# Keys of the last sixteen chunks transposed in blocks by VectorE, another form of the activation, and input buffers of its own for the fourth chunk

## The chip, the cores and the metric

One core of one Trainium2 chip runs the kernel. The metric is the device time of an execution in microseconds: the median of three runs of the kernel before is 521.48 us (521.38 to 521.93). Engines are named as in the profile: PE is TensorE (matmul; PEld is its weight load), DVE is VectorE, ACT is ScalarE, POOL is GpSimd, SP is SyncE, which issues all DMAs here. L452 is line 452 of the kernel.

## The reference

Two stages. For each of 4 batches and 8 heads a recurrence runs over 768 steps with a state of 48x48; its outputs, 3072 tokens of 384 values, go through two matrices of 384x2048 and 2048x384 with the activation h * tanh(softplus(h)) between them.

```python
f = 1.0 / (1.0 + np.exp(-f_logit))
for t in range(S):
    state = f[:, :, t, :, None] * state + np.einsum('bhd,bhe->bhde', k[:, :, t], v[:, :, t])
    y[:, :, t] = np.einsum('bhd,bhde->bhe', q[:, :, t], state)
...
h = x @ w_in
sp = np.where(h > 20.0, h, np.log1p(np.exp(np.minimum(h, 20.0))))
g = h * np.tanh(sp)
return (g @ w_out).astype(np.float32)
```

## The kernel before, in words

**Attention.** The recurrence is done in 24 chunks of 128 steps; chunk n is of batch n % 4. Heads are padded to 64 and lie in four pairs (`NP`), so keys, queries and decays of a chunk are each a tile of 128 partitions (two heads) by 4 x 128. A chunk goes through four steps. `load` and `prep` (L363 to L408) fetch decays, keys, queries and values by four DMAs of 256 KB, turn the decay logits into cumulative sums (by matmuls with a triangle, L391, for chunks 0 to 3, by a scan on VectorE, L396, for the others) and scale keys and queries. `attn0` makes the scores inside half chunks (L427). `attn1` (L446) transposes the scaled keys, four 128x128 transposes on TensorE into a bank of PSUM (L452) and a copy by ScalarE into `kt` (L455). `attn2` (L457) multiplies the transposed keys by the values (L470), keys as the weights, 32 matmuls of 64x64 in four tiles of the array (16 in the last four chunks), and adds that to the state; from chunk 4 on the scores follow in the same step of TensorE. `attn3` (L490) makes the outputs (L505, L517) and splits them into a high part and a low part in `xt`. For chunks 0 to 3 the low part is made by subtracting the high part in PSUM with a matmul (L546) and copying the rest by ScalarE (L548); for the others by a VectorE subtraction (L550). Some rows of `xt` are then moved to other partitions by DMA (L556).

Input buffers come in rings of three (`NR`), chunk n uses number n % 3. So the loads of chunk 3 wait until chunk 0 has been through.

**The two matrices.** Four chunks make a group of 512 tokens. A unit is one group and one of 16 slices of 128 hidden values: 96 units. A unit has 9 matmuls of 512 columns for h (L247, weights and x each as high and low part), the activation, and two units later 9 matmuls (L270) into three accumulators `o`. The first two groups are done in half turns of 8 slices each (`TURNS`), with their sums kept in DRAM between; the weights arrive as 64-bit numbers, are put together by integer operations and split into two parts in `split_w` (L342 to L360), 8 slices before unit 8, the other 8 from unit 16 on.

**The activation** (`mish`, L253) works on 128x512 values. With u = exp(h), taken as exp(10 - relu(10 - h)), it forms n = u(u + 2) and h * n / (n + 2), the division as exp(-ln(n + 2)): relu, exp, ln, exp and a copy for the high part on ScalarE, three operations on VectorE (L259, L260, L263), the low part on GpSimd (L265).

**Order.** Nothing is issued in program order. `Plan` collects all steps with an engine, an estimated cost, what they read and write, and for DMAs a size. `order` packs them by these estimates, with ranks from a backward pass, and applies a fixed list of random nudges to the ranks (`SEEDS`); then each engine gets its instructions in the order of the planned starts, SP's DMAs too. An engine takes its queue strictly in that order. `attend_goal` (with `LEAD`) says which attention steps are put in beside which unit: chunks 4 to 7 beside units -4 to 4, chunks 8 to 11 beside units 24 to 32, and from there four chunks beside each 16 units. Until the first output step TensorE gets fill matmuls (L339) where the plan has it idle. At the end a check (L593) counts decays that are too small; if there are any, a slow version runs behind it, which is not executed with these inputs.

Of the kernel before, what the change touches and what calls it, by code (L numbers as in the profile page):

```python
# [35 lines left out]
H_CAP = 10.0  # L36
# [11 lines left out]
]  # L48
NR = 3
LAG = 2  # L50


class Plan:
# [12 lines left out]
    def add(self, engine, cost, issue, reads=(), writes=(), size=0, port=False):  # L66
# [11 lines left out]
        self.steps.append((engine, cost, issue, before, size, port or engine == "pool"))  # L78

    def pack(self, rank, ahead, haste, back=False):  # L80
# [19 lines left out]
        for _ in range(count):  # L100
# [21 lines left out]
            for a in after[i]:  # L122
                f = a if back else i
                if engine[i] == engine[a] == "pe":
                    lag = 0.0
                else:
                    lag = self.LATENCY[engine[f]]
                    if back and engine[f] == "sp":
                        lag += steps[f][4] / 0.32
# [73 lines left out]
def recurrence_moe_kernel(  # L203
# [29 lines left out]
    two = ctile([P, 1], F32, "two")  # L233
    hcap = ctile([P, 1], F32, "hcap")
# [40 lines left out]
    with tc.tile_pool(name="work", bufs=1) as pool, tc.tile_pool(  # L275
# [17 lines left out]
        at_, h_, o_ = (ring(nm, n, [P, GT], F32, psum) for nm, n in (("at", 3), ("h", 2), ("o", NK)))  # L293
        halves = [dram.tile([DM, GT], F32, tag=f"half{g}", name=f"half{g}") for g in range(2)]
# [14 lines left out]
        def consts():  # L309
# [6 lines left out]
            nc.gpsimd.memset(two, 2.0)  # L316
            nc.gpsimd.memset(hcap, H_CAP)
            nc.gpsimd.memset(ones, 1.0)

# [42 lines left out]

        def load(n, parts):  # L363
            i = n % NR
            st = NP // parts
            for s in range(0, NP, st):
                for nm, dst, src in (("l", l_, ft if n < NS else fl), ("k", k_, kk), ("q", q_, qq)):
                    add("sp", 500, lambda dst=dst, src=src, s=s: nc.sync.dma_start(  # L368
                        dst[i][:, s : s + st], src[n][:, s : s + st]),
                        (), pairs((nm, i), range(s, s + st)), 65.5 * st)  # L370
            add("sp", 500, lambda: nc.sync.dma_start(v_[i], vn[n]), (), [("v", i)], 262)

        def prep(n, parts):
            i = n % NR

            taken[n] = b, keys = banks()
            f, k, q, end = l_[i], k_[i], q_[i], ends[:, n]
            st = NP // parts
            for s0 in range(0, NP, st):
# [3 lines left out]
                kf, kk_, kq = (pairs((x, i), ps) for x in "lkq")  # L383
# [21 lines left out]
                times(0 < n < 2 * GC, w, k[:, s], k[:, s], inv, ki, kk_, port=n < 2 * GC)  # L405
# [410 lines left out]
```

## Time and profile before

| | |
|---|---|
| median of 3 runs | 521.48 us (521.38 to 521.93) |
| span of the profiled execution, from first to last instruction | 519.1 us |
| outside the span, against the median | 2.4 us |
| mean granted clock of TensorE | 0.992 |
| busy: TensorE, VectorE, ScalarE, GpSimd | 505.9, 366.7, 416.4, 156.1 us |
| DMA | 48.86 MB, 94 GB/s |

The profiled execution's own time is its span and what lies before the first and behind the last instruction; the runs that were timed lie within 0.55 us of each other. Matmuls are pipelined, and their ends in the profile are modelled, so the steps between starts, as the chain of waits has them, say more than a matmul's own duration: a matmul of 512 columns is shown with some 400 ns, but nine of them follow each other in 2.10 us.

### The profile page before, as it was taken

Reading aid. Unit: us, or ns where it says so; the run is one execution under the profiler, and the core shown is the slowest. Engines: PE = TensorE matmul, PEld = TensorE weight load, DVE = VectorE, ACT = ScalarE, POOL = GpSimd, SP = SyncE. Lnnn points to the kernel's source line nnn. Section 1 sums busy time; section 2 is a strip of 40 time slices with the busy share of each in tenths; the row PEclk is TensorE's granted clock in tenths of the full one; section 3 lists DMA queues with packets and bytes.
Section 4 is the critical chain, followed back from the end, with each engine's and each line's share of the span. In section 5 each row is a group of like instructions: output and inputs, shape, how many; then the busy total and the mean of one; then the engine's idle time right before and its main releaser. Section 6 shows DMA issues by size and latency. Waiting matters only on the chain.

```text
span 519.1 us, 12812 instructions
## 1 busy us (share of the span) xinstructions
PE 505.9 (97%) x5250; PEld 399.9 (77%) x5250; DVE 366.7 (71%) x592; ACT 416.4 (80%) x731; POOL 156.1 (30%) x134
## 2 busy tenths in 40 slices
PE   8799999999999999999999999999999999999995
PEld 6677777777787778778778778778787787878884
DVE  3679999999997876856767667665668564545451
ACT  6698988988999888888778788877778786777771
POOL 1142443333332223232233232323232221232322
PEclk9799999999999999999999999999999999999999
DMA  8977634524601533320213321130210000010001
GB/s 257 346 227 265 218 125 152 158 87 142 221 25 38 189 102 111 124 59 27 82 40 92 104 82 43 45 101 10 74 49 1 4 2 32 2 60 0 1 1 66
DMA packets 22625, 48.86 MB, mean 94 GB/s; under 512 B 2656, under 2 KB 3808, under 8 KB 22560
## 3 DMA queue, kind: packets, MB, share of 16 engines
q1 hardware_dynamic: 22560, 47.98, 28.2%
q8 instruction: 42, 0.69, 0.5%
q14 instruction: 23, 0.19, 0.1%
HBM read 39.32 MB, written 6.29 MB: 88 GB/s over the span
## 4 chain that ended last, share of the span: by engine, by line
PE 85%; DVE 5%; ACT 3%; DMA 2%; issue 2%; SPq 1%; POOL 0%; DVEq 0%; ACTq 0%
PE h L247 37%; PE o L270 36%; PE at L517 2%; PE at L505 2%; PE at L470 2%; PE at L427 2%; PE at L452 2%; DMA raw<-ww 1%; DMA l<-fl 1%; DVE wt L356 1%; SPq L368 1%; PE o L339 1%; DVE n L259 1%; DVE wt L354 1%; DVE g L263 1%
## 5 line engine op out<-in xcount | busy, mean ns | idle before, releaser
L265 POOL TENSOR_TENSOR gl<-g,gh 128x512 fp32r<-128x512 f32 x96 | 128.9, 1344 | 292.9 <-ACT gh L264 257.0
L247 PE MATMUL h<-xt,wh 128*128 128x512 f32 x576 | 185.0, 402 | 1.2 <-DVE g L263 1.2
L247 PEld LDWEIGHTS h<-xt,wh 128*128 128x128 f32 x576 | 105.2, 188 | 27.7 <-DVE g L263 2.9
L270 PE MATMUL o<-gh,wh 128*128 128x512 f32 x288 | 116.0, 403 | 0.0
L247 PE MATMUL h<-xt,wl 128*128 128x512 f32 x288 | 113.7, 395 | 0.0
L270 PE MATMUL o<-gh,wl 128*128 128x512 f32 x288 | 113.7, 395 | 0.0
L270 PE MATMUL o<-gl,wh 128*128 128x512 f32 x288 | 113.7, 395 | 0.0
L259 DVE SCALAR_TENSOR_TENSOR n<-n 128x512 f32<-128x512 f32 x96 | 67.9, 707 | 54.6 <-ACT n L258 54.2
L257 ACT ACTIVATE n<-h,hcap 128x512 f32<-128x512 f32 x96 | 65.7, 685 | 32.6 <-PE h L247 31.9
L263 DVE TENSOR_TENSOR g<-g,h 128x512 f32<-128x512 f32 x96 | 65.4, 682 | 36.8 <-ACT h L262 36.2
L261 ACT ACTIVATE h<-n,two 128x512 f32<-128x512 f32 x96 | 65.9, 686 | 18.6 <-DVE g L260 17.5
L264 ACT ACTIVATE gh<-g 128x512 fp32r<-128x512 f32 x96 | 60.1, 627 | 19.3 <-DVE g L263 14.1
L260 DVE TENSOR_TENSOR g<-h,n 128x512 f32<-128x512 f32 x96 | 66.2, 690 | 9.3 <-POOL gl L265 1.3
L258 ACT ACTIVATE n<-n,hcap 128x512 f32<-128x512 f32 x96 | 69.2, 721 | 2.3
L270 PEld LDWEIGHTS o<-gh,wh 128*128 128x128 f32 x288 | 54.0, 187 | 13.7 <-issue 0.3
L270 PEld LDWEIGHTS o<-gl,wh 128*128 128x128 f32 x288 | 54.0, 187 | 13.2
L247 PEld LDWEIGHTS h<-xt,wl 128*128 128x128 f32 x288 | 54.0, 187 | 13.2
L270 PEld LDWEIGHTS o<-gh,wl 128*128 128x128 f32 x288 | 54.1, 188 | 12.0
L262 ACT ACTIVATE h<-h 128x512 f32<-128x512 f32 x96 | 55.8, 582 | 1.7
L396 DVE TENSOR_TENSOR_SCAN cum<-go,l 128x512 f32<-128x512 f32 x20 | 26.9, 1343 | 0.9 <-ACT l L388 0.8
L433 DVE TENSOR_TENSOR a<-at,causal 128x256 f32<-128x256 f32 x44 | 17.6, 418 | 10.5 <-PE at L427 10.5
L533 POOL TENSOR_TENSOR state<-tmp,ends 128x256 f32<-128x256 f32 x20 | 16.0, 802 | 24.8 <-PE at L505 16.9
(103 smaller groups left out, 500.6 us busy)
## 6 DMA issues: line engine op xcount, KB each, us to landing
raw<-ww SPq DMA_DIRECT2D x16, 768.0 KB, 4.9
v<-vn SPq DMA_DIRECT2D x24, 256.0 KB, 3.7
k<-kk SPq DMA_DIRECT2D x23, 256.0 KB, 3.0
q<-qq SPq DMA_DIRECT2D x23, 256.0 KB, 3.7
l<-fl SPq DMA_DIRECT2D x20, 256.0 KB, 2.7
out<-ob SPq DMA_DIRECT2D x18, 256.0 KB, 2.9
xt<-xt SPq DMA_DIRECT2D x15, 128.0 KB, 2.1
half<-ob SPq DMA_DIRECT2D x6, 256.0 KB, 2.2
```

The source lines that it names most:

```text
L247: nc.tensor.matmul(h, w[:, j, a * P : (a + 1) * P], xt[:, x, a, :], start=(n == 0), stop=(n == 3 * NK - 1))
L257: ("act", T_ACT(GT, True, 1), 0, lambda: nc.scalar.activation(u, h, AF.Relu, bias=hcap, scale=-1.0)),
L258: ("act", T_ACT(GT, False, 1), 0, lambda: nc.scalar.activation(u, u, AF.Exp, bias=hcap, scale=-1.0)),
L259: ("dve", T_DVE(GT), 1, lambda: nc.vector.scalar_tensor_tensor(n, u, 2.0, u, ALU.add, ALU.mult)),
L260: ("dve", T_DVE(GT), 0, lambda: nc.vector.tensor_tensor(g, h, n, ALU.mult)),
L261: ("act", T_ACT(GT, False, 1), 0, lambda: nc.scalar.activation(h, n, AF.Ln, bias=two)),
L262: ("act", T_ACT(GT, True), 0, lambda: nc.scalar.activation(h, h, AF.Exp, scale=-1.0)),
L263: ("dve", T_DVE(GT), 0, lambda: nc.vector.tensor_tensor(g, g, h, ALU.mult)),
L264: ("act", T_ACT(GT), 0, lambda: nc.scalar.activation(gh, g, AF.Copy)),
L265: ("pool", T_POOL(GT), 1, lambda: nc.gpsimd.tensor_tensor(gl, g, gh.bitcast(F32), ALU.subtract)),
L270: nc.tensor.matmul(o, w[:, j, m * P : (m + 1) * P], x, start=(first and i == 0), stop=(last and i == 2))
L396: add("dve", 2 * T_DVE(w) - 70, lambda s=s, cum=cum: nc.vector.tensor_tensor_scan(cum.rearrange("p a c -> p (a c)"), go[:, s].rearrange("p ...
```

## The change

- From chunk 8 on (`TD`), `attn1` has VectorE transpose the keys in blocks of 32x32 into the tile `inv` (free by then), stores that to DRAM (`kd`) and loads it back into `kt` by four DMAs, one for every 32 steps, each of 128 runs of 512 bytes. In `kt` the channels of a pair now lie four values (16 bytes) apart, and the update reads them so (`mixed`). The four transposes on TensorE and the ScalarE copy go for these chunks.
- The activation is h * (1 - 2r) with r = 1 / ((1 + u)^2 + 1): exp, clamp and add 1, square, ln, exp, one product. The product made is h * (r - 0.5), and the factor -2 is applied where the accumulators `o` are copied or added. The square is done by ScalarE for units 0 to 29 and by VectorE from unit 30 on (`SQ_DVE`).
- Chunk 3 is loaded into `ob` (output buffers) and one of the `g` tiles, and from chunk 4 on the ring starts anew with buffer 0 (`slot`, `place`).
- The low parts of chunks 0 to 3 are made by VectorE as those of the others (`LO_PE` is empty).
- The steps are packed anew, with a list of 24 nudges in place of 48. A step can have a lag of its own; none has one.

The core of the diff:

```diff
-H_CAP = 10.0
+U_CAP = 22026.46484375
...
 SEEDS = [
...
 NR = 3
+LO_PE = ()
+K_POOL = (1, 2, 3, 4, 5, 6, 7)
 LAG = 2
+TD = 8
+SQ_DVE = range(30, 96)
...
-    def add(self, engine, cost, issue, reads=(), writes=(), size=0, port=False):
+    def add(self, engine, cost, issue, reads=(), writes=(), size=0, port=False, lag=None):
...
-    def mish(h, n, g, gh, gl):
-
-        u = n
+    def mish(h, n, g, gh, gl, on_dve=False):
+
+
+        square = (
+            ("dve", T_DVE(GT), 1, lambda: nc.vector.tensor_tensor(n, n, n, ALU.mult)) if on_dve else
+            ("act", T_ACT(GT), 0, lambda: nc.scalar.activation(n, n, AF.Square))
+        )
         return (
-            ("act", T_ACT(GT, True, 1), 0, lambda: nc.scalar.activation(u, h, AF.Relu, bias=hcap, scale=-1.0)),
-            ("act", T_ACT(GT, False, 1), 0, lambda: nc.scalar.activation(u, u, AF.Exp, bias=hcap, scale=-1.0)),
-            ("dve", T_DVE(GT), 1, lambda: nc.vector.scalar_tensor_tensor(n, u, 2.0, u, ALU.add, ALU.mult)),
-            ("dve", T_DVE(GT), 0, lambda: nc.vector.tensor_tensor(g, h, n, ALU.mult)),
-            ("act", T_ACT(GT, False, 1), 0, lambda: nc.scalar.activation(h, n, AF.Ln, bias=two)),
-            ("act", T_ACT(GT, True), 0, lambda: nc.scalar.activation(h, h, AF.Exp, scale=-1.0)),
-            ("dve", T_DVE(GT), 0, lambda: nc.vector.tensor_tensor(g, g, h, ALU.mult)),
+            ("act", T_ACT(GT, True), 0, lambda: nc.scalar.activation(n, h, AF.Exp)),
+            ("dve", 70 + GT / 1.92, 1, lambda: nc.vector.tensor_scalar(n, n, U_CAP, 1.0, ALU.min, ALU.add)),
+            square,
+            ("act", T_ACT(GT, False, 1), 0, lambda: nc.scalar.activation(n, n, AF.Ln, bias=ones)),
+            ("act", T_ACT(GT), 0, lambda: nc.scalar.activation(n, n, AF.Exp, scale=-1.0)),
+            ("dve", T_DVE(GT), 0, lambda: nc.vector.scalar_tensor_tensor(g, n, half_, h, ALU.subtract, ALU.mult)),
             ("act", T_ACT(GT), 0, lambda: nc.scalar.activation(gh, g, AF.Copy)),
             ("pool", T_POOL(GT), 1, lambda: nc.gpsimd.tensor_tensor(gl, g, gh.bitcast(F32), ALU.subtract)),
         )
...
+        kd_ = [dram.tile([P, GT], F32, tag=f"kd{i}", name=f"kd{i}") for i in range(2)]
...
-            nc.gpsimd.memset(two, 2.0)
-            nc.gpsimd.memset(hcap, H_CAP)
             nc.gpsimd.memset(ones, 1.0)
+            nc.scalar.activation(half_, ones, AF.Ln, bias=ones)
...
+        def slot(n):
+            return n if n < NR else (n - GC) % NR
+
+        def place(n):
+            if n == NR:
+                return [x.rearrange("p (a c) -> p a c", a=NP) for x in ob_] + [g_[1]], [("ob", m) for m in range(NK)] + [("g", 1)]
+            i = slot(n)
+            return [l_[i], k_[i], q_[i], v_[i]], [(x, i) for x in "lkqv"]
+
         def load(n, parts):
-            i = n % NR
+            (l, k, q, v), (kl, kk_, kq, kv) = place(n)
             st = NP // parts
             for s in range(0, NP, st):
-                for nm, dst, src in (("l", l_, ft if n < NS else fl), ("k", k_, kk), ("q", q_, qq)):
+                for key, dst, src in ((kl, l, ft if n < NS else fl), (kk_, k, kk), (kq, q, qq)):
                     add("sp", 500, lambda dst=dst, src=src, s=s: nc.sync.dma_start(
-                        dst[i][:, s : s + st], src[n][:, s : s + st]),
-                        (), pairs((nm, i), range(s, s + st)), 65.5 * st)
-            add("sp", 500, lambda: nc.sync.dma_start(v_[i], vn[n]), (), [("v", i)], 262)
+                        dst[:, s : s + st], src[n][:, s : s + st]),
+                        (), pairs(key, range(s, s + st)), 65.5 * st)
+            add("sp", 500, lambda: nc.sync.dma_start(v, vn[n]), (), [kv], 262)
...
-                times(0 < n < 2 * GC, w, k[:, s], k[:, s], inv, ki, kk_, port=n < 2 * GC)
+                times(n in K_POOL, w, k[:, s], k[:, s], inv, ki, kk_, port=n < 2 * GC)
...
-            k = k_[n % NR]
+            (_, k, _, _), (_, kn, _, _) = place(n)
 
             def transposes():
                 for p in range(NP):
                     nc.tensor.transpose(b[:, p, :], k[:, p, :], ident)
 
-            add("pe", 400, transposes, pairs(("k", n % NR)), [key])
-            add("act", T_ACT(GT, True), lambda: nc.scalar.activation(kt_[n % 2], b, AF.Copy), [key], [("kt", n % 2)])
+            if n >= TD:
+                tr, t = inv_[n % 2].rearrange("x p c -> x (p c)"), ("tr", n % 2)
+                add("dve", T_DVE(GT), lambda: nc.vector.transpose(
+                    tr.rearrange("x (c d p) -> x p c d", c=4, p=NP), k.rearrange("x p (c d) -> x p c d", c=4)), pairs(kn), [t])
+                add("sp", 500, lambda: nc.sync.dma_start(kd_[n % 2], tr), [t], [("kd", n % 2)], 262)
+                for c in range(4):
+                    add("sp", 500, lambda c=c: nc.sync.dma_start(
+                        kt_[n % 2][32 * c : 32 * c + 32].rearrange("x p c -> x (p c)").rearrange("x (r d) -> x r d", r=4),
+                        kd_[n % 2].rearrange("(r x) (c d) -> c x r d", r=4, c=4)[c]), [("kd", n % 2)], [("kt", n % 2, c)], 65.5)
+                return
+
+            add("pe", 400, transposes, pairs(kn), [key])
+            add("act", T_ACT(GT, True), lambda: nc.scalar.activation(kt_[n % 2], b, AF.Copy), [key], [("kt", n % 2, c) for c in range(4)])
...
+            kt, kts = kt_[n % 2], [("kt", n % 2, c) for c in range(4)]
+            mixed = kt.rearrange("x p c -> x (p c)").rearrange("x (c p) -> x p c", p=NP)
...
                     for c in range(2 - last):
                         for e in range(2):
                             c0 = (2 * p + e) * 64
+                            w = kt[half(c), p, half(e)] if n < TD else mixed[half(c), p, half(e)]
                             nc.tensor.matmul(
-                                u[c][half(e), p, :], kt_[n % 2][half(c), p, half(e)], v[half(c), c0 : c0 + 64], start=True, stop=True
+                                u[c][half(e), p, :], w, v[half(c), c0 : c0 + 64], start=True, stop=True
                             )
...
-                add("pe", 1208, lambda: [update(), scores()], [("kt", n % 2), ("v", n % NR)] + reads,
+                add("pe", 1208, lambda: [update(), scores()], kts + [vk] + reads,
...
             add("pe", 1100 if first else 1340, outputs,
-                pairs(("q", i)) + [("st", batch), ("mid", n % 2), ("v", i), ("a", n % 2, 0), ("a", n % 2, 1)], keys)
+                pairs(qn) + [("st", batch), ("mid", n % 2), vk, ("a", n % 2, 0), ("a", n % 2, 1)], keys)
...
-                if n < GC:
+                if n in LO_PE:
...
-                        add("dve", T_DVE(GT), lambda m=m: nc.vector.tensor_tensor(ob_[m], o_[m], ob_[m], ALU.add),
+                        add("dve", T_DVE(GT), lambda m=m: nc.vector.scalar_tensor_tensor(
+                            ob_[m], o_[m], -2.0, ob_[m], ALU.mult, ALU.add),
                             [("o", m)], pairs(("ob", m)))
                     elif m == 1:
-                        add("act", T_ACT(GT, True), lambda m=m: nc.scalar.activation(ob_[m], o_[m], AF.Copy),
+                        add("act", T_ACT(GT, True), lambda m=m: nc.scalar.activation(ob_[m], o_[m], AF.Copy, scale=-2.0),
                             [("o", m)], pairs(("ob", m)))
                     else:
 
-                        add("dve", T_DVE(GT), lambda m=m: nc.vector.tensor_copy(ob_[m], o_[m]),
+                        add("dve", T_DVE(GT), lambda m=m: nc.vector.tensor_scalar(ob_[m], o_[m], -2.0, None, ALU.mult),
...
-                ops = mish(h, n_[us], g_[us], gh_[gs], gl_[gs])
+                ops = mish(h, n_[us], g_[us], gh_[gs], gl_[gs], u in SQ_DVE)
                 rw = (
-                    ([kh], [kn]), ([], [kn]), ([], [kn]), ([kh, kn], [kg]), ([kn], [kh]), ([], [kh]),
-                    ([kh], [kg]), ([kg], [("gh", gs)]), ([kg, ("gh", gs)], [("gl", gs)]),
+                    ([kh], [kn]), ([], [kn]), ([], [kn]), ([], [kn]), ([], [kn]),
+                    ([kh, kn], [kg]), ([kg], [("gh", gs)]), ([kg, ("gh", gs)], [("gl", gs)]),
```

## Rows read from the trace of the kernel before

**Rows 1.** Busy us (instructions) by stretch and engine; last granted clock, DMA share, GB/s.

```profile
0.00:45.00 45.00, 39.36 (x768) 30.81 (x769) 29.57 (x54) 34.24 (x75) 12.87 (x21) 0.92 0.83 276
45.00:101.40 56.40, 54.87 (x634) 42.28 (x634) 55.47 (x86) 50.66 (x89) 19.70 (x14) 1.00 0.52 171
101.40:513.10 411.70, 411.66 (x3850) 326.80 (x3849) 281.62 (x454) 330.92 (x569) 123.50 (x99) 1.00 0.20 63
```

**Rows 2.** The chain of waits from 160 to 184 us: start us, us, what.

```profile
163.06 0.44 PE at L452 x4
163.50 2.10 PE h L247 x9
165.60 0.62 PE at L470 x32
...
166.69 2.30 PE o L270 x9
...
170.23 2.30 PE h L247 x9
```

**Rows 3.** Busy time by stretch, line 452 alone.

```profile
45.00:101.40 56.40, 1.85 (x12) 1.41 (x12) 1.00 0.52 171
101.40:513.10 411.70, 8.97 (x60) 7.45 (x60) 1.00 0.20 63
```

**Rows 4.** Busy time from 45 to 101.4 us, of line 247, then of line 270.

```profile
45.00:101.40 56.40, 26.06 (x100) 18.37 (x101) 1.00 0.52 171
...
45.00:101.40 56.40, 20.55 (x81) 14.80 (x81) 1.00 0.52 171
```

**Rows 5.** Instructions by line and shape: out<-in, shape, count, busy us, mean ns, idle before.

```profile
L258 ACT ACTIVATE n<-n,hcap 128x512 f32<-128x512 f32 x96 | 69.2, 721 | 2.3
L259 DVE SCALAR_TENSOR_TENSOR n<-n 128x512 f32<-128x512 f32 x96 | 67.9, 707 | 54.6 <-ACT n L258 54.2
L260 DVE TENSOR_TENSOR g<-h,n 128x512 f32<-128x512 f32 x96 | 66.2, 690 | 9.3 <-POOL gl L265 1.3 <-DVE n L259 0.5
L261 ACT ACTIVATE h<-n,two 128x512 f32<-128x512 f32 x96 | 65.9, 686 | 18.6 <-DVE g L260 17.5 <-DVE flag L600 1.0
L257 ACT ACTIVATE n<-h,hcap 128x512 f32<-128x512 f32 x96 | 65.7, 685 | 32.6 <-PE h L247 31.9
L263 DVE TENSOR_TENSOR g<-g,h 128x512 f32<-128x512 f32 x96 | 65.4, 682 | 36.8 <-ACT h L262 36.2
L264 ACT ACTIVATE gh<-g 128x512 fp32r<-128x512 f32 x96 | 60.1, 627 | 19.3 <-DVE g L263 14.1 <-PE o L270 3.8 <-PE h L247 0.8
L262 ACT ACTIVATE h<-h 128x512 f32<-128x512 f32 x96 | 55.8, 582 | 1.7
...
L354 DVE SCALAR_TENSOR_TENSOR wt<-raw,wt 128x768 int32<-128x768 int32 x16 | 16.7, 1041 | 0.0
...
L359 DVE TENSOR_TENSOR wl<-wt,wh 128x768 fp32r<-128x768 f32 x16 | 16.2, 1014 | 0.0
...
L470 PEld LDWEIGHTS at<-v,kt 64*64 64x64 f32 x704 | 13.4, 134 | 8.8 <-issue 2.5 <-ACT gh L264 1.1 <-ACT h L262 1.1
...
L386 DVE TENSOR_SCALAR l<-l 128x512 f32<-128x512 f32 x23 | 11.1, 488 | 1.0 <-DMA l<-ft 0.7 <-DMA l<-fl 0.2
...
L517 PEld LDWEIGHTS at<-a,v 64*32 64x32 f32 x704 | 6.7, 108 | 1.7 <-issue 0.2
```

**Rows 6.** DMA issues by line: KB of each, median us to landing.

```profile
half<-ob SPq DMA_DIRECT2D x6, 256.0 KB, 2.2
...
xt<-xt SPq DMA_DIRECT2D x3, 96.0 KB, 5.2
```

**Rows 7.** ScalarE in order of time, near 25 us.

```profile
25.02 0.66 ACT L548 ACTIVATE xt<-at 128x256 fp32r<-128x256 f32 x2 [0.37 <-PE at L546]
```

**Rows 8.** TensorE in order of time, two places of the front.

```profile
25.76 1.05 PE L391 MATMUL at<-tri,l 128*128 128x128 f32 x8
...
45.29 0.82 PE L247 MATMUL h<-xt,wh 128*128 128x512 f32 x2
```

More of the change, by code (lines that the diff above doesn't have):

```diff
@@ L77, in add @@
         before.discard(n)
-        self.steps.append((engine, cost, issue, before, size, port or engine == "pool"))
+        lag = self.LATENCY[engine] if lag is None else lag
+        self.steps.append((engine, cost, issue, before, size, port or engine == "pool", lag))
     def pack(self, rank, ahead, haste, back=False):
@@ L126, in pack @@
                 else:
-                    lag = self.LATENCY[engine[f]]
+                    lag = steps[f][6]
                     if back and engine[f] == "sp":
@@ L232, in recurrence_moe_kernel @@
     causal = ctile([P, CH], F32, "causal")
-    two = ctile([P, 1], F32, "two")
-    hcap = ctile([P, 1], F32, "hcap")
+    half_ = ctile([P, 1], F32, "half")
     ones = ctile([P, 1], F32, "ones")
@@ L315, in consts @@
             nc.scalar.activation(minus, ident, AF.Copy, scale=-1.0)
-            nc.gpsimd.memset(two, 2.0)
-            nc.gpsimd.memset(hcap, H_CAP)
             nc.gpsimd.memset(ones, 1.0)
+            nc.scalar.activation(half_, ones, AF.Ln, bias=ones)
+            nc.scalar.activation(half_, half_, AF.Exp, scale=-1.0)
         nc.vector.memset(state0, 0.0)
@@ L360, in split_w @@
                 wl[:, j], w, wh[:, j].bitcast(F32), ALU.subtract), [kt, ("w", "h", j)], [("w", "l", j)], port=True)
+        def slot(n):
[5 more added lines that the diff above has]
+            return [l_[i], k_[i], q_[i], v_[i]], [(x, i) for x in "lkqv"]
         def load(n, parts):
-            i = n % NR
+            (l, k, q, v), (kl, kk_, kq, kv) = place(n)
             st = NP // parts
             for s in range(0, NP, st):
-                for nm, dst, src in (("l", l_, ft if n < NS else fl), ("k", k_, kk), ("q", q_, qq)):
+                for key, dst, src in ((kl, l, ft if n < NS else fl), (kk_, k, kk), (kq, q, qq)):
                     add("sp", 500, lambda dst=dst, src=src, s=s: nc.sync.dma_start(
-                        dst[i][:, s : s + st], src[n][:, s : s + st]),
-                        (), pairs((nm, i), range(s, s + st)), 65.5 * st)
-            add("sp", 500, lambda: nc.sync.dma_start(v_[i], vn[n]), (), [("v", i)], 262)
+                        dst[:, s : s + st], src[n][:, s : s + st]),
+                        (), pairs(key, range(s, s + st)), 65.5 * st)
+            add("sp", 500, lambda: nc.sync.dma_start(v, vn[n]), (), [kv], 262)
         def prep(n, parts):
-            i = n % NR
+            (f, k, q, _), names = place(n)
+            end = ends[:, n]
             taken[n] = b, keys = banks()
-            f, k, q, end = l_[i], k_[i], q_[i], ends[:, n]
             st = NP // parts
@@ L382, in prep @@
                 w = st * C
-                kf, kk_, kq = (pairs((x, i), ps) for x in "lkq")
+                kf, kk_, kq = (pairs(x, ps) for x in names[:3])
                 dec, kd = b[s0 // st][:, 0:w].rearrange("p (a c) -> p a c", a=st), [keys[s0 // st]]
@@ L415, in attn0 @@
         def attn0(n, parts):
-            k, q = k_[n % NR], q_[n % NR]
+            (_, k, q, _), (_, kn, qn, _) = place(n)
             b, keys = taken[n]
@@ L436, in reads @@
             def reads(s):
-                return pairs(("k", n % NR), range(s, s + st)) + pairs(("q", n % NR), range(s, s + st))
+                return pairs(kn, range(s, s + st)) + pairs(qn, range(s, s + st))
             if n >= GC:
@@ L459, in attn2 @@
             st, ks = state[:, n % B], ("st", n % B)
-            v = v_[n % NR]
+            (*_, v), (*_, vk) = place(n)
             u = [x[:, c : c + NP * 64].rearrange("p (a c) -> p a c", a=NP) for x, c in ((at1, 0), (at_[1], NP * 64))]
@@ L480, in attn2 @@
             else:
-                add("pe", 745, update, [("kt", n % 2), ("v", n % NR)], keys[: 2 - last])
+                add("pe", 745, update, kts + [vk], keys[: 2 - last])
             if n < B:
@@ L490, in attn3 @@
         def attn3(n):
-            i = n % NR
-            q, v = q_[i], v_[i]
+            (_, _, q, v), (_, _, qn, vk) = place(n)
             first, batch = n < B, n % B
@@ L744, in recurrence_moe_kernel @@
                         moe_out(o[m], m, gh, gl, 0, True, True, *(w[:, :, NK * P :] for w in wj))
-                        nc.vector.tensor_tensor(total_o[:, m], total_o[:, m], o[m], ALU.add)
+                        nc.vector.scalar_tensor_tensor(total_o[:, m], o[m], -2.0, total_o[:, m], ALU.mult, ALU.add)
                 nc.sync.dma_start(out.rearrange("(m p) t -> p m t", p=P)[:, :, tok], total_o)
```

3 lines of the change are left out of this document (added), and 5 rows, old and new, of the table SEEDS.

## The prediction

> **What bounds the kernel now.** I read the busy time by stretch first [rows 1]. From 101.4 to 513.1 us TensorE is busy for 411.66 of 411.70 us at full clock, with VectorE at 68% and ScalarE at 80%: here every us of TensorE work is a us of the kernel, and another engine's work costs nothing until TensorE waits for it. Before that it is different. From 45 to 101.4 us VectorE is busy for 55.47 of 56.40 us and ScalarE for 50.66; up to 45 us nothing is full. Next comes the chain of waits in the middle of the run [rows 2]: it is TensorE alone, and the steps between its pieces give the price of each attention block. The busy time of single lines by stretch [rows 3, 4] says how much work falls where, the lines by shape [rows 5] what one instruction takes. Behind 513.1 us only the last output's copy and store are left, some 6 us.
>
> The profiled execution spans 519.1 us; the three runs have their median at 521.48 us, so 2.4 us lie outside the span. I subtract from 521.5. A measurement of this kernel can tell 0.2%, or 1 us, from no change.
>
> **Key transposes off TensorE.** Four transposes standing alone take 0.44 us of the chain, from 163.06 to 163.50 us [rows 2]. Chunks 8 to 23 are 16 such groups: 60 of their 64 matmuls fall behind 101.4 us, and the 12 of the middle stretch include the other four [rows 3]. 16 x 0.44 = **7.0 us** less, with no TensorE work in their place.
>
> What replaces them is, for each chunk, one VectorE transpose of 128x512. No row shows one. The bounds are 488 ns (one operand, line 386) and twice the 707 ns of line 259; I take 0.7 us, as most operations of this size do [rows 5]. 16 x 0.7 = 11 us, where VectorE has 130 us idle [rows 1]: nothing on the path. Then come a store of 256 KB and four loads of 64 KB. A 256 KB store takes 2.2 us to land, the slowest small move between partitions 5.2 us [rows 6], so with the issues on SP the keys are ready some 7 to 10 us after VectorE starts, against about 1 us now. On SP the store waits for VectorE and the loads for the store; queued behind them are input loads, weight loads, the xt moves and output stores. Chunks 12 to 23 go four to 16 units of 2 x 2.10 us [rows 2], so one in 16.8 us; chunks 8 to 11 go four to 8 units, one in 8.4 us. There are two buffers of each kind, so the trip hides; if that cover is gone, the update (line 470) waits for the keys and all of TensorE behind it. ScalarE loses 16 copies.
>
> **The transposed keys as weights.** In the update the 64 weight columns now lie 16 bytes apart, where they were neighbours: 12 x 32 + 4 x 16 = 448 loads, in 112 rounds of four tiles. Update and scores together take 1.09 us for 64 matmuls, from 165.60 to 166.69 us [rows 2], so 68 ns a round. A load of 64 columns takes 134 ns and one of 32 takes 108 ns [rows 5], so 0.81 ns a column and 52 ns for 64, which just fits in a round. No row shows a weight load with spaced columns. The bounds: nothing below, since spaced columns can't be read faster than neighbours, and above four times the column time, 208 ns, my guess of the worst from this row. The nearest rows for spacing are the integer operations of the weight split: line 354 reads words 8 bytes apart and takes 1041 ns for 768 elements, line 359 reads neighbours and takes 1014 ns [rows 5]. They lie by the lower end, so I take 0 and keep the upper end for the rivals. The Trainium skill, SBUF — State Buffer, section Door 1: The DMA port swizzle (why `[64,N]` ≈ `[32,N]`), says that SBUF is read in lines of 16 bytes, that full bandwidth needs at least two accesses to a line, and that each step to a new line costs; it gives no price. At 8 bytes the trace agrees; 16 bytes would be on the dear side of that rule, and no row here has such a step in a long read.
>
> **The activation.** Removed for each unit: 685 + 721 + 686 + 582 ns on ScalarE and 707 + 690 + 682 ns on VectorE. Added on ScalarE: an exp out of PSUM (582, as line 262), a square (627, as line 264), a logarithm with a bias (721, as line 258) and an exp (627), so 2557 for 2674 ns, and 1930 from unit 30 on, where VectorE squares. Added on VectorE: clamp and add (488) and the last product (707), so 1195 for 2079 ns, and 1885 from unit 30 on [rows 5]. Behind 101.4 us all this lies under TensorE. Between 45 and 101.4 us some eleven units are activated: VectorE loses 11 x 0.88 = 9.7 us and stands at 46, ScalarE loses 1.3 and stands at 49.4 of 56.4 us. TensorE's need there is 181 matmuls [rows 4] at 2.10 / 9 us, 42.2 us, and the attention of three chunks: 0.44, 1.09 and 1.24 us, with 0.2 us more behind each of the last two, where the next nine matmuls take 2.30 us [rows 2]; 3.2 us a chunk, 9.5 us. That is 51.7 of 56.4 us, so **4.7 us** are lost. With VectorE relieved TensorE is the next limit and ScalarE close behind it at 49.4, so I take 3.0 us back, between 0 and 4.7.
>
> **The start.** The low parts of the first four chunks no longer go through TensorE (line 546) and ScalarE (line 548), but through one VectorE subtraction. In the trace the copies of line 548 for chunk 1 wait 0.37 us for line 546, take 0.66 us and end at 25.68 us [rows 7]; the cumulative sums of chunk 3, in the same banks, start at 25.76 us [rows 8]. The subtraction can run beside the first copies, so I estimate 0.8 of these 1.03 us gained, and half of it once more at the end of chunk 3. The fourth chunk's loads no longer wait for chunk 0, nor hold up SP's queue, and chunks 4 and up get their buffers one chunk sooner; since DMA's share is 0.83 and ScalarE is busy for 34.24 of 45 us [rows 1], I count only 0.8 us for it, **2.0 us** together. The whole order is packed anew, so the bounds are 2 us lost (the first unit, now at 45.29 us [rows 8], starts later) and 6 us gained, what lies idle of ScalarE in this stretch being 10.8. The factor -2 rides on copies that exist already, the last one included: 0.
>
> Sum: 521.5 - 7.0 - 3.0 - 2.0 = **509.5 us**. With the bounds of the two front terms: 521.5 - 7.0 - 4.7 - 6 = 503.8 to 521.5 - 7.0 + 2 = 516.5 us.
>
> **Rivals.**
> - The front gives nothing: ScalarE takes VectorE's place as the limit, or the new order wastes what is freed. For it speaks ScalarE's 90% of the stretch [rows 1]; against it that VectorE is the fuller by 4.8 us. 521.5 - 7.0 = 514.5 us.
> - Half rate: spaced columns load in 104 ns, some 52 ns more a round, 112 x 0.052 = 5.8 us, so 515.3 us. For it: a load has little slack in its round. Against it: the 8-byte rows.
> - **Slower**: the same load at the upper bound, 208 ns. A round of 68 ns grows by about 144 ns with the load's overhead; 112 x 0.144 = 16.1 us, so 525.6 us. It decides from the point where it eats the 12.0 us gained: 107 ns a round, or columns at three times their time. Its place is the update of every chunk from 8 on.
> - Late keys: the updates of chunks 8 to 11, and the units that need a group's last chunk, wait 0.6 us each for the trip through DRAM, some 8 times: 5 us, 514.5 us. Against it: two buffers, and an order that counts with a delay for SP.
> - The transposes go and the time stays, because they stood in TensorE's waits: behind 101.4 us only 0.04 us of waits exist [rows 1], so no chance.
>
> **How the numbers follow.** Forecast 0.52 (504 to 513 us), the front gives nothing 0.16, half rate 0.18, late keys 0.04, slower 0.10. The first four lie between 504 and 517 us; half rate together with a poor start would pass 517.5 and is a small part of its 0.18. So the range is 504.5 to 517.5 us, which leaves out the slower rival and thin tails. Slower by over 0.2%: 0.11, the rival and a sum of bad ends; within 0.2%: 0.03; faster: 0.86.
>
> **What would show it.** Right: line 452 with 32 matmuls for 96; TensorE without waits from about 95 us on; update and scores still near 1.09 us; VectorE well under 98% in the front with ScalarE near 95%; the first unit at 43 to 44 us. Half rate would show as an update and scores block of about 1.5 us, the slower rival as one of over 2 us, late keys as TensorE idle ahead of line 470. The forecast is wrong if the update grows, or if the stretch up to full TensorE stays as long as it is.

## The result, and the profile after

The changed kernel takes 513.39 us (median of 4 runs, 512.51 to 514.10) against 521.43 us of the kernel before on the same chip: a ratio of 0.984, 95% interval 0.982 to 0.987, or 8.0 us. The forecast was 509.5 us with a range of 504.5 to 517.5. The profiled execution took 513.55 us and spans 511.8.

The number lies in the range, but its sum does not hold: the two terms of the front together came out at nothing, the spaced weights took back what the transposes gave, and a term that the sum did not have is as large as the whole gain. First the rows that answer to those of before. Busy time by stretch (columns: length, then PE, PEld, DVE, ACT and POOL with instructions, granted clock, DMA share, GB/s):

```profile
0.00:45.00 45.00, 39.53 (x838) 31.40 (x839) 33.54 (x67) 33.38 (x74) 12.68 (x20) 1.00 0.83 290
45.00:101.40 56.40, 51.48 (x620) 40.34 (x620) 55.02 (x80) 49.99 (x89) 20.87 (x15) 1.00 0.54 187
101.40:505.40 404.00, 402.31 (x3722) 326.70 (x3721) 270.43 (x441) 275.08 (x481) 134.95 (x98) 1.00 0.25 81
```

Against [rows 1], TensorE is idle for more of the middle stretch, 4.9 us for 1.5, and VectorE is as full as it was. The chain of waits (start us, us, what), to be held against [rows 2]:

```profile
157.64 2.04 PE h L249 x9
159.68 1.11 PE at L500 x32
160.79 0.47 PE at L442 x32
161.26 2.29 PE o L275 x9
```

Nine matmuls of 512 columns take 2.04 us and not 2.10, which no step of the change explains. The update (line 500) takes 1.11 us where it took 0.62. TensorE has no transposes (line 467) behind 101.4 us. The weight loads of the update take 185 ns on the mean, for 134 [rows 5]; that mean still holds the loads of chunks 0 to 7, whose columns are neighbours, and the median, which is a spaced load, is 212 ns. VectorE's transpose takes 1104 ns. Line 467 by stretch, then instructions by line and shape, then the loads' shortest, median and longest time:

```profile
101.40:505.40 404.00, 0.00 (x0) 0.00 (x0) 1.00 0.25 81
```

```profile
L268 DVE SCALAR_TENSOR_TENSOR g<-n,half,h 128x512 f32<-128x512 f32 x96 | 71.1, 741 | 54.9 <-ACT n L267 52.1 <-POOL gl L270 2.8
L264 DVE TENSOR_SCALAR n<-n 128x512 f32<-128x512 f32 x96 | 49.2, 512 | 49.5 <-ACT n L263 49.4
L500 PEld LDWEIGHTS at<-v,kt 64*64 64x64 f32 x672 | 20.8, 185 | 10.5 <-issue 7.3 <-ACT kt L481 2.5 <-ACT l L402 0.3
L471 DVE STREAM_TRANSPOSE inv<-k 128x512 f32<-128x512 f32 x16 | 17.7, 1104 | 0.3
```

```profile
L500 PEld LDWEIGHTS at<-v,kt x672: 129/212/215, 11.1 to 418.9; 64*64 64x64 f32 x168
```

The first unit starts 5 us earlier than in [rows 8] (TensorE in order of time):

```profile
40.32 0.81 PE L249 MATMUL h<-xt,wh 128*128 128x512 f32 x2
```

Some of the 5 us may be TensorE's clock, which was granted at 0.92 of full speed up to 45 us in the trace before [rows 1] and at 1.00 here. Most of it is not: the kernel before with a pad (below) was granted 0.96 there, and its first unit starts at 45.38 us.

But between 40 and 140 us TensorE now waits 6.5 us, where before it waited 1.6 (what TensorE waited for in that stretch: us in total, times, longest; before, then after):

```profile
PE h L247 <- DVE g L263: 1.2, 3, 0.6
PE at L452 <- POOL k L306: 0.4, 1, 0.4
```

```profile
PE h L249 <- DVE g L268: 5.5, 6, 1.5
PE at L500 <- ACT kt L481: 1.0, 1, 1.0
```

### The profile page after: what moved, and what is told of

It is laid out like the page before. It is cut to its first block, busy times and chain, and to the rows that moved or that the text cites. A ratio compares the mean times of both kernels' runs of the same rounds, so it can differ in the third digit from the quotient of the medians.

```text
span 511.8 us, 12578 instructions
## 1 busy us (share of the span) xinstructions
PE 493.3 (96%) x5178; PEld 398.4 (78%) x5178; DVE 359.0 (70%) x586; ACT 359.1 (70%) x643; POOL 168.5 (33%) x132
## 4 chain that ended last, share of the span: by engine, by line
PE 75%; DVE 13%; ACT 7%; issue 3%; DMA 2%; DVEq 0%; ACTq 0%
PE o L275 33%; PE h L249 31%; PE at L500 4%; DVE wl L365 2%; PE at L534 2%; DVE wt L362 2%; PE at L546 2%; DVE wt L360 2%; DVE g L268 2%; PE at L442 2%; DMA raw<-ww 1%; DVE wt L359 1%; DVE n L264 1%; ACT wt L357 1%; DVE q L312 1%
## 5 line engine op out<-in xcount | busy, mean ns | idle before, releaser
L270 POOL TENSOR_TENSOR gl<-g,gh 128x512 fp32r<-128x512 f32 x96 | 143.7, 1500 | 296.4 <-ACT gh L269 262.3
L249 PE MATMUL h<-xt,wh 128*128 128x512 f32 x576 | 180.8, 395 | 5.6 <-DVE g L268 5.5
L268 DVE SCALAR_TENSOR_TENSOR g<-n,half,h 128x512 f32<-128x512 f32 x96 | 71.1, 741 | 54.9 <-ACT n L267 52.1
L266 ACT ACTIVATE n<-n,ones 128x512 f32<-128x512 f32 x96 | 69.4, 723 | 51.9 <-DVE n L259 51.3
L264 DVE TENSOR_SCALAR n<-n 128x512 f32<-128x512 f32 x96 | 49.2, 512 | 49.5 <-ACT n L263 49.4
L263 ACT ACTIVATE n<-h 128x512 f32<-128x512 f32 x96 | 56.7, 591 | 38.0 <-PE h L249 37.5
L267 ACT ACTIVATE n<-n 128x512 f32<-128x512 f32 x96 | 60.4, 629 | 2.1
L259 DVE TENSOR_TENSOR n<-n 128x512 f32<-128x512 f32 x66 | 47.2, 715 | 1.8
L500 PEld LDWEIGHTS at<-v,kt 64*64 64x64 f32 x672 | 20.8, 185 | 10.5 <-issue 7.3
L500 PE MATMUL at<-v,kt 64*64 64x64 f32 x672 | 24.1, 265 | 2.6 <-ACT kt L481 1.4
```

The lines of the kernel that those rows point to most:

```text
L249: nc.tensor.matmul(h, w[:, j, a * P : (a + 1) * P], xt[:, x, a, :], start=(n == 0), stop=(n == 3 * NK - 1))
L259: ("dve", T_DVE(GT), 1, lambda: nc.vector.tensor_tensor(n, n, n, ALU.mult)) if on_dve else
L263: ("act", T_ACT(GT, True), 0, lambda: nc.scalar.activation(n, h, AF.Exp)),
L264: ("dve", 70 + GT / 1.92, 1, lambda: nc.vector.tensor_scalar(n, n, U_CAP, 1.0, ALU.min, ALU.add)),
L267: ("act", T_ACT(GT), 0, lambda: nc.scalar.activation(n, n, AF.Exp, scale=-1.0)),
L268: ("dve", T_DVE(GT), 0, lambda: nc.vector.scalar_tensor_tensor(g, n, half_, h, ALU.subtract, ALU.mult)),
```

## The experiments

All times are medians. The kernel before measured 521.4 to 522.2 us beside the five groups of runs, so versions of different groups are compared by their times, with some 0.5 us of doubt.

### Where the tiles start

I looked into the 2.04 us first. The change takes two 4-byte constants out and puts one in. Each takes a slot of 32 bytes ahead of all working tiles, so xt, gh and gl, which TensorE streams through the weights, moved by 32 bytes (the weights lie ahead of these constants and stayed): in the kernel before they start 32 bytes behind a multiple of 64, in the changed one at a multiple of 128. A constant that nothing reads shifts them:

```diff
     flag = ctile([1, 1], I32, "flag")
+    pad = ctile([P, 1], F32, "pad")
```

In the kernel before (64 bytes behind a multiple of 128):

> The kernel before with one more constant of 4 bytes (it takes 32), so that all work tiles, the moving operands xt, gh and gl among them, start at a multiple of 64 bytes as they do after the change; the order and all work are unchanged. Theory: the 512-column matmuls follow each other in 226.7 ns when the moving operand starts at a multiple of 64 bytes and in 233.3 ns when it starts 32 bytes behind one. Then nine take 2.04 us for 2.10 us, and the some 1550 of them behind 101 us save 1550 x 6.6 ns = 10 us: 511 us, faster than the changed kernel. Rival: the pace comes with the new activation, which no longer writes its logarithm and exponential into the PSUM bank of h; then this kernel stays at 521.4 us with 2.10 us for nine.

In the changed kernel (32 bytes behind a multiple of 64, as before the change):

> The changed kernel with one more constant, so that the work tiles start 32 bytes behind a multiple of 64 as they did before. Theory of the start address: nine matmuls take 2.10 us again, and the time is about 513.4 + 9 = 522 us, no gain over the kernel before. Rival (the activation makes the pace): 513.4 us with 2.04 us for nine.

Measured: 515.88 us (ratio 0.989, 0.985 to 0.993) and 521.08 us (1.000, 0.998 to 1.002). Their chains:

```profile
160.45 2.06 PE o L271 x9
162.51 0.44 PE at L453 x4
162.95 2.08 PE h L248 x9
165.03 0.62 PE at L471 x32
```

```profile
158.55 2.10 PE h L250 x9
160.65 1.12 PE at L501 x32
```

At the start that the kernel before has, the whole change is worth nothing. Its measured gain is the start of the tiles, which came by chance, with a constant. The kernel before, given the pad, gains less than was expected, at 2.06 us for nine matmuls and not 2.04. Two things could be the rest: 64 against 128, or the old activation's writes into PSUM, which are gone in the new one. The changed kernel with two pads tells them apart:

```diff
+    pad = ctile([P, 1], F32, "pad")
+    pad2 = ctile([P, 1], F32, "pad2")
```

> The changed kernel with two unused 4-byte constants, so that its tiles start 64 bytes behind a multiple of 128; unpadded they start at a multiple of 128, and in the kernel before with one constant added, which ran its 512-column matmuls at a median of 229.0 ns, 64 bytes behind one. Nothing else changes. Theory 'the remaining 2.3 ns are the start at 64 against 128': median pace 229 ns, mean 229.3, so 1.6 ns x 1728 = 2.8 us more than the changed kernel: 516.2 us (515 to 517.5). Rival 'they are the old activation's writes of h into PSUM, and any multiple of 64 will do': median 227 ns, mean 227.7, and 513.4 us (512.5 to 514.3).

```profile
154.94 2.06 PE o L277 x9
157.00 2.06 PE h L251 x9
```

It took 514.89 us (514.68 to 516.95): the pace is that of the other kernel at this start (mean 229.3 ns from one matmul's start to the next in both), so the start decides and the activation does not. The time is a little under the expected range. The three starts give means of 233.3, 229.3 and 227.7 ns (steps with a wait or other work between left out). Some 1386 of the 1728 matmuls start behind 140 us, where TensorE no longer waits: 1386 x 5.6 ns = 7.8 us, and 521.08 - 513.39 = 7.7 us are measured.

### Spaced weight columns

The changed kernel, with the same loads and the same order, reads its weights from neighbouring addresses, then from 8 bytes apart. Both read other channels than they should, so they give a time and not the result. The first edit:

```diff
-mixed = kt.rearrange("x p c -> x (p c)").rearrange("x (c p) -> x p c", p=NP)
+mixed = kt
```

> The changed kernel, where the state update of chunks 8 to 23 reads its 64 weight columns as neighbours in kt and not 16 bytes apart. It reads other channels than it should, so the output is not the reference's; every instruction, its order, its wait and its DMA stay as they are. Theory 'the spacing is the price': the weight loads of those blocks fall from 185 to about 134 ns, the update's 32-matmul step on the chain from 1.11 to about 0.62 us, and since TensorE sets the end from 140 us on, the time falls by about 0.49 us x 12 and half of that x 4, some 7 us: 506.5 us (505 to 508.5). Rival 'the source is the price' (kt written by a DMA in four pieces, the block waits or reads slower for that): loads stay at 185 ns and the time at 513.4 us (512.5 to 514.3). Rival 'shorter but covered' (other waits take the freed time): loads at 134 ns and a time of 511 to 513.4 us.

> As the one before, with the weight columns 8 bytes apart in place of 4 or 16 (again other channels than it should read, and the same instructions, order and DMAs). Theory 'cost grows with the distance': 185 ns at 16 bytes and 134 at 4 put 8 bytes near 151 ns, the step near 0.78 us and the time near 509 us (508 to 510.5). Rival 'two words in 16 bytes are free': 134 ns, 0.62 us and 506.5 us, as for neighbours. Rival 'whatever is not a neighbour is slow': 185 ns, 1.11 us and 513.4 us.

Measured: 505.98 us (505.08 to 506.81; ratio 0.971, 0.968 to 0.973) and 506.80 us (505.66 to 507.42). The step of the chain and the weight loads, for neighbours and then for 8 bytes:

```profile
159.31 0.62 PE at L500 x32
```

```profile
L500 PEld LDWEIGHTS at<-v,kt 64*64 64x64 f32 x672 | 13.0, 134 | 9.4 <-issue 7.3 <-ACT kt L481 1.4 <-ACT l L402 0.3
```

```profile
160.10 0.64 PE at L500 x32
```

```profile
L500 PEld LDWEIGHTS at<-v,kt 64*64 64x64 f32 x672 | 13.2, 135 | 11.0 <-issue 7.7 <-ACT kt L481 2.5 <-ACT l L402 0.3
```

So the spacing costs 513.39 - 505.98 = 7.4 us, as much as the transposes were worth, and not in proportion to the distance: 8 bytes are nearly free, 16 are not. That is what the Trainium skill, SBUF — State Buffer, section Door 1: The DMA port swizzle (why `[64,N]` ≈ `[32,N]`), says of lines of 16 bytes that need two accesses each for full bandwidth, and here the trace agrees. The same section also says that four fp32 can be stepped over for free; 212 against 135 ns, the medians at 16 and at 8 bytes, speaks against that, and the measurement decides.

Can the keys be had as neighbours? The transposed key must be spread over DRAM in runs of 128 bytes for it. Three versions differ in who cuts the runs. First the loads, 16 a chunk in place of four:

> The changed kernel with the transposed keys laid out so that the 64 weight columns are neighbours again (VectorE writes runs of 32 neighbours, each of the four loads becomes four loads of runs of 128 bytes in the same step); the order is unchanged. Theory: weight columns 16 bytes apart load at about half rate and make the update longer by some 0.5 us in 12 chunks and by half of it in 4; the loads go back from 185 to 134 ns, and the time falls by about 7 us to 506 us. Rival: the update is longer because the keys come late; then the loads stay long or TensorE waits ahead of them, more with sixteen loads than with four, and the time stays at 513 us or grows.

Then the store, four a chunk in place of one, the four loads whole rows (its edit, shortened):

```diff
-tr.rearrange("x (c d p) -> x p c d", c=4, p=NP), k...
+tr.rearrange("x (c p d) -> x p c d", c=4, p=NP), k...
-nc.sync.dma_start(kd_[n % 2], tr)
+[nc.sync.dma_start(kd_[n % 2].rearrange("(d a) (b r x) -> r d a b x", a=4, b=NP, r=4)[r],
+    tr[32 * r : 32 * r + 32].rearrange("y (a b x) -> y a b x", a=4, b=NP)) for r in range(4)]
-    kt_[...].rearrange("x (r d) -> x r d", r=4), kd_[n % 2].rearrange("(r x) (c d) -> c x r d", r=4, c=4)[c])
+    kt_[...], kd_[n % 2].rearrange("(d a) f -> a d f", a=4)[c])
```

> The changed kernel with its keys placed so that the weights of the state update are neighbours: VectorE's transpose writes neighbours, the store to DRAM is four DMAs (one for each 32 partitions, in runs of 128 bytes) in place of one, and the four loads fetch whole rows of 2 KB. The computation is the reference's, the planned order the same. Theory: it gets what the neighbours are worth, 506.5 us (505 to 509), with weight loads near 134 ns, the transpose on VectorE at 0.71 in place of 1.10 us, and four stores that land in 2 to 3 us ahead of their need. Rival 'late keys': sixteen small loads a chunk made TensorE wait 23 us in all in an earlier run; if three more issues a chunk on SP or 128-byte runs do the same in part, TensorE's first update matmul waits for the load of kt by 0.5 us or more a chunk, and the time is 513 us or above.

And that one with a single load of 256 KB for the four:

> The version with neighbouring weights and four stores of 128-byte runs, its four loads a chunk made one load of 256 KB (128 rows of 2 KB): eight issues a chunk on SP become five, as in the changed kernel. Theory 'late keys by SP's queue': there five chunks' update blocks were 0.4 to 1.3 us longer than the 1.29 us of the others, on the wait for kt's DMAs, 3 us in all; with three issues a chunk fewer the keys come in time and the run stands near that with wrong channels, 506 to 507 us. Rival 'late by the transfer': one load of 256 KB lands later than four of 64 KB, or the stores' short runs are what is late; the blocks stay longer and the time at 509 to 511 us.

Measured: 555.01 us, **509.52 us** (509.25 to 510.30; ratio 0.977, 0.974 to 0.980) and 532.09 us (531.39 to 536.45). What TensorE waited for in the first; in the second the same, then its weight loads and VectorE's transpose, then its DMAs (KB, median us to landing); in the third the waits, then one chunk's trip in the chain:

```profile
PE at L500 <- DMA kt<-kd: 23.1, 17, 3.0
```

```profile
PE at L503 <- DMA kt<-kd: 2.0, 4, 1.1
```

```profile
L503 PEld LDWEIGHTS at<-v,kt 64*64 64x64 f32 x672 | 14.0, 134 | 11.9 <-issue 7.2 <-DMA kt<-kd 1.8 <-ACT kt L484 1.4
...
L471 DVE STREAM_TRANSPOSE inv<-k 128x512 f32<-128x512 f32 x16 | 11.3, 709 | 0.3
```

```profile
kd<-inv SPq DMA_DIRECT2D x64, 64.0 KB, 2.2
kt<-kd SPq DMA_DIRECT2D x64, 64.0 KB, 2.0
```

```profile
PE at L503 <- DMA kt<-kd: 22.9, 13, 3.2
```

```profile
274.56 2.15 DMA kd<-inv
...
276.73 5.33 DMA kt<-kd
```

The second version beats both kernels. It has the neighbours' 134 ns, and still gives back 3.5 us of the 7.4; 2.0 us of that are waits for keys that land late, the rest is not settled. The third was to mend that by fewer issues and made it far worse: the theory of SP's queue fell. Its rival named the load, but was off by far in the time (509 to 511 us). In the chunk at 275 us the one load lands after 5.33 us (4.9 to 5.8 us in the eleven that the chain shows), where the second version's four small ones land some 2.0 us behind their issue; why a load of 256 KB takes longer was not tried further. So the trip through DRAM has little cover to spare. In the trace of the changed kernel the last load of a chunk lands 0.8 to 4.2 us ahead of the update.

In the first and the third the waits are not the whole loss. In their profiled executions, which span 554.5 and 534.4 us, the mean granted clock is 0.961 and 0.981, for 0.996 and 0.995 in the changed kernel and the second version. If TensorE had work all the while, that is an estimated 554.5 x 0.035 = 19.4 us in the first, beside 23.1 us of waits, and 534.4 x 0.014 = 7.5 us in the third.

### The other parts, and the order

The transposes back on TensorE, all else as changed (`TD = 24`):

> The changed kernel with all key transposes on TensorE and ScalarE as before (the limit is set to 24 chunks), all else as changed, packed anew. Theory: 16 transposes cost 7.0 us and the update with neighbouring columns gives 7.5 us back, so about 513 us, within 2 us for the new order. Rival, the prediction: the transposes off TensorE were worth their 7 us, so this one is at 520 us.

Measured: 527.50 us (ratio 1.011). The planner packs another order for it. The steps are as they should be, but TensorE waits behind 140 us (below, the longest three), where the changed kernel has no wait:

```profile
174.43 0.44 PE at L467 x4
174.87 2.09 PE h L249 x9
176.96 0.62 PE at L500 x32
```

```profile
PE at L467 <- DVE k L312: 1.9, 1, 1.9
PE h L249 <- DVE g L268: 1.7, 1, 1.7
PE o L275 <- POOL gl L270: 1.1, 2, 0.6
```

By its steps, 0.44 + 0.62 against 1.11 us, it would stand where the changed kernel does. It stands 14 us above. Its first unit starts 3.4 us later, at 43.73 us; it waits 5.9 us behind 140 us; and its granted clock is 0.988 for 0.996, an estimated 526.0 x 0.008 = 4 us. How much of that is the new order, and how much the transposes, which wait for their keys themselves, the run can't tell: it is inconclusive. The kernel before with the new activation alone is packed anew too:

> The kernel before with the new activation alone (its constants, its output factor and its square on VectorE from unit 30); with two constants gone and one added its tiles start at multiples of 64 bytes, as in the run of the kernel before with one constant added (515.9 us, 229.0 ns for a 512-column matmul). Its order is packed anew. Theory 'the old activation's two writes of h into PSUM from ScalarE slow the matmuls': the pace falls to 226.7 to 227.7 ns, worth 1.3 to 2.3 ns x 1728 = 2.2 to 4.0 us. Theory 'a relieved VectorE saves in the front': 3 us more, so 509 to 511 us with both. Rival 'the activation is worth nothing, the pace comes from elsewhere in the change': 229 ns and 515 to 517 us.

Measured: 517.49 us (516.62 to 518.88), behind the 515.88 us of the old activation at a worse start. Its first unit starts at 44.75 us and TensorE waits 4.1 us for the product of line 266 to free h. So an activation that takes 0.83 us a unit off VectorE up to unit 29 (741 + 512 ns in the rows of the changed kernel, for 707 + 690 + 682 [rows 5]) shows no gain here. How much is luck of the order? The changed kernel with the other list of trial numbers, nothing else:

```diff
-    11000009, 11000043, ...
+    10000067, 10000086, ...
```

> The changed kernel with the planner's list of trial numbers of the kernel before, nothing else: the same instructions, in another order that the planner found as good by its own costs. It tells how much of a time is the order. Theory 'the order is worth several us': the packed-anew runs so far lost 3 to 13 us to waits of TensorE in the front; 516 to 528 us. Rival 'orders are alike': 512 to 515 us, and then those runs owe their time to their edits.

Measured: 529.33 us (526.87 to 532.32; ratio 1.016, 1.011 to 1.021), just above the range of the theory. Between 40 and 140 us:

```profile
PE h L251 <- DVE g L270: 6.6, 3, 4.4
PE at L536 <- DVE a L450: 2.1, 1, 2.1
PE h L251 <- DVE wl L367: 0.8, 1, 0.8
```

The same instructions in another order, and 16 us; the profiled execution is 13.3 us longer than that of the changed kernel. Its first unit starts at 41.53 us, 1.2 later; it waits 3.0 us more in this stretch, and 2.2 us behind it. The clock adds to that. Behind the wait of 4.4 us TensorE was granted half its clock (1.2 GHz) up to 93.0 us, and the same stands behind waits of 2.1 us, from 62.2 us on, and 1.9 us, from 215.8 us on. Below are the first unit and the matmuls behind the wait of 4.4 us, then a stretch with its granted clock of 0.51:

```profile
41.53 0.81 PE L251 MATMUL h<-xt,wh 128*128 128x512 f32 x2
...
89.15 0.91 PE L251 MATMUL h<-xt,wh 128*128 128x512 f32 x2 [4.40 <-DVE g L270]
```

```profile
89.60:93.00 3.40, 3.40 (x13) 2.18 (x11) 2.18 (x3) 1.81 (x4) 1.29 (x1) 0.51 0.80 244
```

By the mean granted clock, 0.988 for 0.996, that is an estimated 525.1 x 0.008 = 4 us. So order, waits and clock make up 10 to 11 of the 13.3 us; the rest is not settled. No version that is packed anew can be read for a few us. The last run keeps the order and takes VectorE work out of the front:

```diff
-lambda: nc.vector.tensor_scalar(t, t, 3, None, ALU.logical_shift_left), (), [kt], port=True)
+lambda: None, (), [kt], port=True)
```

> The changed kernel without one VectorE instruction of each of the 16 weight splits (the shift of wt in place, 644 ns on the mean); the split weights are other numbers for it. Order, waits and all other instructions stay. It tells whether VectorE sets the pace of the front. Theory 'VectorE bounds the front': 13 of the 16 lie ahead of 140 us, 13 x 0.64 = 8.4 us less on VectorE there; what TensorE waits there (6.8 us after 60 us, 5.5 of it the first product's matmul that waits for VectorE's last step of the activation) goes, 4 to 7 us: 506.5 to 509.5 us. Rival 'something else bounds it, or the order': TensorE waits as long as before, 512 to 514 us. In between, 509.5 to 512: half of each.

Measured: 511.98 us (511.41 to 513.23), nearer the rival. From 40 to 140 us:

```profile
PE h L249 <- DVE g L268: 5.1, 5, 2.1
```

16 instructions less, some 10 us of VectorE, bring 1.4 us. So the amount of VectorE's work alone does not set the length of the front. That VectorE holds it by the order of its work is not excluded, since it is still busy for 34.08 us of the 35 from 45 to 80 us:

```profile
45.00:80.00 35.00, 32.24 (x482) 25.03 (x481) 34.08 (x48) 32.20 (x60) 12.48 (x11) 1.00 0.63 221
```

## Why the number was right and the sum was not

| Step | Predicted, us | In the runs, us |
|---|---|---|
| Transposes off TensorE | -7.0 | 16 steps of 0.44 gone from the chain: -7.0, counted, not measured alone |
| Spaced weight columns | 0 (up to +16.1) | +7.4 |
| Start of the first unit | -2.0 | 5.0 earlier: -5.0 |
| VectorE relieved, 45 to 101.4 us | -3.0 | TensorE's waits up to 140 us 4.9 longer: +4.9 |
| Start of the tiles | not in the sum | -7.7 |
| Sum | -12.0 | -7.4, measured -8.0 |

**Transposes.** Right by the trace: no matmul of line 467 behind 101.4 us, and no step of 0.44 us in the chain. No run isolates it, but two things bear it out. Behind the first unit the two traces hold the same TensorE instructions, but for 64 transposes less and two fill matmuls more. And the run at the old start closes on it: by its own trace its first unit starts at 40.84 us, 4.5 earlier, and it waits 5.0 us for 1.6, so -7.0 + 7.4 - 4.5 + 3.4 = -0.7, measured -0.6 us.

**Spaced columns.** This step failed. "They lie by the lower end, so I take 0" rested on VectorE rows at 8 bytes; the columns lie at 16, and at 8 TensorE too reads nearly for free. The half-rate rival named place and size: an update and scores of about 1.5 us and 5.8 us in all, against 1.11 + 0.47 us and 7.4. A spaced load takes 77 ns more than one of neighbours (212 for 135), where half rate had 52 and the slower rival 156. The rows bore out the rule only on the side where it costs nothing, and that was no reason to take nothing on the other.

**The front.** The step "4.7 us are lost", with 3.0 of them taken back, failed. It came from adding up what TensorE should need, 51.7 us. But [rows 1] had TensorE busy for 54.87 of 56.40 us, with 1.6 us of waits. Of the busy time 2.36 us are nine fill matmuls (line 339), which the sum of the need left out:

```profile
45.00:101.40 56.40, 2.36 (x9) 1.26 (x8) 1.00 0.52 171
```

So the ceiling was 1.5 us of idle time, or 3.9 us if all the fill counts as idle. Two engines were full at once, and relief of one could not return more than the other's idle time. It returned nothing: TensorE's waits grew by 4.9 us. What VectorE was freed of it did not keep either: in that stretch the weight splits on it (instructions that write wt, before and after) were 30 for 24, and grew by as much as the 9.7 us that the step took off.

```profile
45.00:101.40 56.40, 21.67 (x24) 1.00 0.52 171
```

```profile
45.00:101.40 56.40, 31.64 (x30) 1.00 0.54 187
```

The start was better than forecast, 40.32 us for 43 to 44. It brought nothing either: TensorE, 5 us ahead, ran into the product that frees h and waited most of it away. The rival "the front gives nothing" was right in its outcome. The first of its two reasons, ScalarE full, was not: ScalarE is busy for 49.99 of 56.40 us. The second, an order that wastes what is freed, fits the rows above, but no run shows it alone. What holds the front is not settled. Another order alone moves the time by more than any step of the sum.

**What was missing.** The predicted gain was 12.0 us. Nothing of it was left: the spaced columns took back what the transposes gave, and longer waits took back the earlier start. The start of the tiles put 7.7 us in its place. So the number came out right by luck, through a term that nobody had weighed. Of the signs announced, an update and scores of about 1.5 us and a front no shorter than before were those named for a wrong forecast, and both appeared.

**Late keys.** Right for the changed kernel, where no wait for kt's DMA appears. That the trip "hides" was too sure: with three issues more, or one larger load, it did not.

## What to carry to other kernels

Before a busy engine is relieved, read the idle time of the one that sets the end in the same stretch: it, with filler work counted as idle, is the ceiling of the gain, whatever the busy share of the other. When an edit adds or drops even a 4-byte constant, compare the pace of untouched matmuls first, and pad both versions to the same start before crediting the edit. Where an order is packed anew, run another packing of the same code; if that moves the time more than the edit should, only edits that keep the order can be read. Where a version makes TensorE wait, read its granted clock beside the waits before the rest is put down to anything else.

## What was not expected of the hardware

- TensorE's pace for 512 fp32 columns hangs on where the streamed tile starts: 233.3 ns at 32 bytes behind a multiple of 64, 229.3 at 64 behind a multiple of 128, 227.7 to 228.0 at a multiple of 128, in two kernels at each start. All working tiles moved together; of what these matmuls read, only the streamed tiles did.
- VectorE's transpose of 128x512 takes 709 ns when it writes neighbours and 1104 ns when it writes 16 bytes apart.
- VectorE's subtraction of the weight split takes 948 ns at the median, and 2065 at worst. Of its 16 executions in the changed kernel, the five that began while GpSimd's subtraction (line 270) ran took 1985 to 2065 ns, and the other eleven 930 to 957 ns. Below, the operation of VectorE and the one of GpSimd beside it in the changed kernel: by the median it would end at 111.78 us, but GpSimd is busy from 110.67 to 112.06, and VectorE ends 0.8 us behind that, at 112.88, as if it had only then begun.

```profile
110.83 2.05 DVE L365 TENSOR_TENSOR wl<-wt,wh 128x768 fp32r<-128x768 f32 x1
```

```profile
110.67 1.39 POOL L270 TENSOR_TENSOR gl<-g,gh 128x512 fp32r<-128x512 f32 x1 [2.78 <-ACT gh L269]
```

The Trainium skill, SBUF — State Buffer, section SBUF: two separate sides, describes this as a lock on a port pair that VectorE and GpSimd share, with the loser blocked until the other is done. The trace agrees in these five places; no run here removed one of the two.
